# First batch's queries and keys in 1 KB runs, window values for four heads per load, other planner numbers

## The chip, the cores and the metric

The kernel runs on one core of one Trainium2 chip. The metric is device time in microseconds (us), lower is better. In this text PE is the tensor engine, ACT the scalar engine, DVE the vector engine, POOL the GpSimd engine, and SP the engine that issues all DMA transfers here. Each engine works through its own queue of instructions in the order in which the program wrote them, and waits at an instruction whose inputs or buffers are not ready.

## The reference

Attention over 2 batches, 8 heads, 576 tokens, 64 features, then two feed-forward layers on all 1152 tokens:

```python
q_d = q.reshape(B, H, Sd, 4, D).mean(axis=3)      # k_d and v_d in the same way
out_up = np.repeat(sm_attn(q_d, k_d, v_d), 4, axis=2)
mask = np.abs(pos[:, None] - pos[None, :]) < 4
scores = np.where(mask, scale * np.matmul(q, k.transpose(0, 1, 3, 2)), -1e9)
out_local = np.matmul(softmax(scores), v)
x = (out_up + out_local) as (1152, 512)
h = x @ w_in;   x = (h * np.tanh(softplus(h))) @ w_out       # 512 -> 2048 -> 512
g = x @ w_gate; x = (silu(g) * (x @ w_val)) @ w_out2         # 512 -> 1536 -> 512
```

The weights arrive as 64-bit numbers and are turned into 32-bit ones on the core.

## The kernel before

**Attention.** Heads are taken in pairs, so there are 8 pairs (b, p) of a batch and two heads. `prep` loads queries and keys of a pair (`qk`, line 419; the last 64 tokens of all heads come in `qr`, line 394), transposes them on PE (L453 and L459) into PSUM, and ACT copies the PSUM bank to `qkT` (L464, recorded under the helper's line L222). DVE sums groups of four tokens into `qkd` (L474). `duo` then takes two units of 192 tokens of a pair: on PE the mask and the local scores (L552, L557) and the scores of the sums (L566); on DVE the maxima (L572, L578, L583); on ACT the exponentials (L590); normalising on DVE and ACT (L597 to L614); transposes back on PE (L622, L632) and their copies on ACT (`pt`, `ptd`); then the products with the values (L652 for the sums, L660 for the windows). Every window of 70 tokens that a unit needs has its values in `vw`, loaded for the two heads of the pair (L528, L536). There are 12 duos: for each of three pieces of 384 tokens the four pairs. The result of a duo is 128 rows of `xt`.

**Feed-forward.** The first product (`l1`, L733 to L735: three products of 32-bit halves) can start on a piece of 384 tokens when the four duos of that piece are done and a weight chunk has been converted on DVE and ACT (L295 to L331). The second product reads `G`, which comes from the first by a chain on ACT and DVE (L786 to L802). The products with 512 columns (L927 to L929) belong to the last layer.

**Order of the work.** `Plan` is a list scheduler that runs when the program is built. Every operation has an engine, a duration in us that only steers the order, and a `want` time; each engine takes, of what its inputs and buffers allow, what is wanted first, and the instructions are written in that order. Where the planner finds PE idle before 95 us it writes a product that nobody reads (`warm`, L1043). So the number and the place of these products are fixed in the program and don't depend on what happens on the chip.

Of the kernel before, what the change touches and what calls it, by code (L numbers as in the profile page):

```python
# [20 lines left out]
WIN = 70  # L21
# [3 lines left out]
RING = 6  # L25
# [3 lines left out]
FLIGHT = 5  # L29
COLD = 4.0  # L30
# [6 lines left out]
# High words of a float64: the smallest and the largest whose value float32 can hold.  # L37
# [4 lines left out]
class Ring:  # L42
    """n places for buffers of one kind; each goes to the next that asks when it is free."""
# [35 lines left out]
class Plan:  # L79
    """Orders the work of the engines: each takes, of what its inputs and buffers allow, what is  # L80
    wanted first. The durations (us) only steer that order; Tile sets every wait. spare: work for
    an idle tensor engine, with its first and last time and its duration."""
# [6 lines left out]
    def add(self, eng, fn, deps=(), want=0.0, new=(), use=(), table=None):  # L89
        """eng: {engine: duration}; fn(engine) emits. new: buffers it takes first; use: others it touches."""  # L90
# [75 lines left out]
def attention_moe_kernel(  # L166
# [21 lines left out]
    # ------------------------------------------------------------ pools  # L188
# [28 lines left out]
    def us_mm(n):  # L217
        return n / 2400 + 0.003
# [14 lines left out]
    def buf(pool, shape, dt, tag, n):  # L233
        """A buffer; make() gives its tile, in the operation that takes it."""
# [23 lines left out]
    # ------------------------------------------------------------ weights  # L258
# [82 lines left out]
    # ------------------------------------------------------------ attention  # L341
# [55 lines left out]
    def prep(b, p, w):  # L397
        """Queries and keys of two heads with features on partitions, sums of 4 tokens of all."""
        qk = buf(ld, [128, 2, 4, 2, 64], F32, "qk", 3)
# [29 lines left out]
        for i in range(2):  # L429
            l_q.append(plan.add({E_SP: us_dma(1024, 256)}, ld_main(i), l_q, w - 12, [] if l_q else [qk], [qk] if l_q else []))  # L430
# [649 lines left out]
```

## Time and profile before

| | |
|---|---|
| runs before | 513.38, 513.72, 514.73 us; median 513.72 |
| span of the profiled execution | 513.0 us, from its first instruction to its last |
| time of the profiled execution | not shown apart from its span; the median run lies 0.7 us above the span |
| PE busy | 506.3 us (99%) |
| DVE, ACT, POOL busy | 378.4 (74%), 289.6 (56%), 22.9 us (4%) |
| granted TensorE clock | 0.999 |

PE shows 99% busy because the products of an engine overlap in the record (each lasts longer than the distance to the next one) and because the products that nobody reads count as busy. What PE does with its time is read from the distance between the starts of products in the timeline.

### The profile page before, as it was taken

How to read it: one execution, taken by the hardware profiler on the slowest of the kernel's cores; microseconds unless marked ns; L12 is line 12 of the kernel's file. 1: busy time of each engine (PE TensorE's matmuls, PEld its weight loads, DVE VectorE, ACT ScalarE, POOL GpSimd, SP SyncE). 2: the span in 40 equal slices, each digit the busy share in tenths (PEclk: the TensorE clock that was granted, in tenths of full speed). 3: DMA queues.
4: the chain of work that ended last, by engine and by line, in shares of the span. 5: the costliest groups of instructions: out<-in, count | busy, mean ns of one | idle time of the engine just before them, and what ended most of it. 6: DMA issues, size and time to landing. Idle time of an engine off the chain costs nothing.

```text
span 513.0 us, 9052 instructions
## 1 busy us (share of the span) xinstructions
PE 506.3 (99%) x3518; PEld 473.5 (92%) x3518; DVE 378.4 (74%) x760; ACT 289.6 (56%) x591; POOL 22.9 (4%) x47
## 2 busy tenths in 40 slices
PE   8999999999999999999999999999999999999997
PEld 6786688999999999999999999999998899998885
DVE  2776899999998999999889896767764198732322
ACT  3898989698899897469542544334433344310000
POOL 4420320000000000000000000000000000000000
PEclk9999999999999999999999999999999999999999
DMA  9975444452132332451303154222222023000022
GB/s 172 196 147 114 109 133 138 129 165 82 45 121 54 118 87 76 161 165 41 99 27 123 60 173 136 82 84 84 82 83 82 1 82 124 1 1 0 1 87 97
DMA packets 58618, 48.24 MB, mean 94 GB/s; under 512 B 31056, under 2 KB 53840, under 8 KB 58576
## 3 DMA queue, kind: packets, MB, share of 16 engines
q1 hardware_dynamic: 58576, 47.68, 33.6%
q8 instruction: 27, 0.44, 0.4%
q14 instruction: 15, 0.12, 0.1%
HBM read 45.31 MB, written 2.36 MB: 93 GB/s over the span
## 4 chain that ended last, share of the span: by engine, by line
PE 97%; ACT 1%; DVE 1%; issue 0%
PE b L733 23%; PE b L734 23%; PE b L735 23%; PE b L929 5%; PE b L927 5%; PE b L928 5%; PE warm L1043 2%; PE b L557 2%; PE b L660 2%; PE b L622 2%; PE b L453 2%; PE b L566 1%; PE b L652 1%; PE b L632 1%; PE b L552 1%; ACT qkT L222 1%
## 5 line engine op out<-in xcount | busy, mean ns | idle before, releaser
L733 PE MATMUL b<-xy,wt 128*128 128x384 f32 x480 | 161.0, 336 | 0.0
L735 PE MATMUL b<-xy,wt 128*128 128x384 f32 x480 | 160.4, 334 | 0.0
L734 PE MATMUL b<-xy,wt 128*128 128x384 f32 x480 | 160.3, 334 | 0.0
L733 PEld LDWEIGHTS b<-xy,wt 128*128 128x128 f32 x480 | 90.1, 188 | 0.6 <-issue 0.2
L734 PEld LDWEIGHTS b<-xy,wt 128*128 128x128 f32 x480 | 90.1, 188 | 0.0
L735 PEld LDWEIGHTS b<-xy,wt 128*128 128x128 f32 x480 | 90.1, 188 | 0.0
L733 PE MATMUL b<-G,wt 128*128 128x384 f32 x192 | 64.1, 334 | 0.0
L734 PE MATMUL b<-G,wt 128*128 128x384 f32 x192 | 64.1, 334 | 0.0
L735 PE MATMUL b<-G,wt 128*128 128x384 f32 x192 | 64.1, 334 | 0.0
L222 ACT ACTIVATE G<-H 128x384 fp32r<-128x384 f32 (+1 forms) x41 | 25.2, 619 | 63.1 <-DVE H L899 40.2
L295 ACT ACTIVATE cw<-raw 128x512 f32<-128x512 f32 x60 | 39.8, 669 | 21.5 <-DVE wt L331 12.1
L331 DVE TENSOR_TENSOR wt<-cw,wt 128x512 fp32r<-128x512 f32 x68 | 46.1, 684 | 1.2
L310 DVE SCALAR_TENSOR_TENSOR cw<-raw,cw 128x512 uint32<-128x512 uint32 x68 | 46.6, 688 | 0.4
L315 DVE SCALAR_TENSOR_TENSOR cw<-raw,cw 128x512 uint32<-128x512 uint32 x68 | 46.3, 684 | 0.4
L899 DVE TENSOR_TENSOR H<-b,H 128x384 f32<-128x384 f32 x36 | 20.0, 557 | 32.8 <-PE b L735 32.2
L929 PE MATMUL b<-wt,G 128*128 128x512 f32 x108 | 42.1, 389 | 0.0
L928 PE MATMUL b<-wt,G 128*128 128x512 f32 x108 | 42.0, 389 | 0.0
L927 PE MATMUL b<-wt,G 128*128 128x512 f32 x108 | 42.0, 389 | 0.0
L942 DVE TENSOR_TENSOR acc<-b,acc 128x512 f32<-128x512 f32 x18 | 12.4, 692 | 34.6 <-PE b L929 34.6
L896 ACT ACTIVATE H<-b 128x384 f32<-128x384 f32 x36 | 17.6, 489 | 34.5 <-PE b L735 34.5
L735 PEld LDWEIGHTS b<-G,wt 128*128 128x128 f32 x192 | 36.0, 188 | 0.0
L734 PEld LDWEIGHTS b<-G,wt 128*128 128x128 f32 x192 | 36.0, 188 | 0.0
(85 smaller groups left out, 783.7 us busy)
## 6 DMA issues: line engine op xcount, KB each, us to landing
raw<-in_moe_w_out_dram SPq DMA_DIRECT2D x28, 512.0 KB
raw<-in_moe_w_in_dram SPq DMA_DIRECT2D x16, 512.0 KB
raw<-in_moe_w_gate_dram SPq DMA_DIRECT2D x12, 512.0 KB
raw<-in_moe_w_val_dram SPq DMA_DIRECT2D x12, 512.0 KB
vq<-in_v_dram SPq DMA_DIRECT2D x8, 288.0 KB
out_dram<-acc SPq DMA_DIRECT2D x9, 256.0 KB
qk<-in_q_dram SPq DMA_DIRECT2D x8, 256.0 KB
qk<-in_k_dram SPq DMA_DIRECT2D x8, 256.0 KB
```

What stands on the lines that cost most here:

```text
L222: ACT.activation(out, in_, AF.Copy)
L295: ACT.activation(cw.tile, h.bitcast(F32), AF.Abs)
L310: DVE.scalar_tensor_tensor(out=c, in0=words()[:, :, 0], scalar=29, in1=c, op0=ALU.logical_shift_right, op1=ALU.bitwise_or)
L315: DVE.scalar_tensor_tensor(out=c, in0=words()[:, :, 1], scalar=0xC0000000, in1=c, op0=ALU.bitwise_and, op1=ALU.bitwise_or)
L331: DVE.tensor_tensor(out=wt.tile[:, 1], in0=cw.tile, in1=wt.tile[:, 0].bitcast(F32), op=ALU.subtract)
L733: PE.matmul(out=ps, lhsT=wt_hi, rhs=m_hi, start=first, stop=False)
L734: PE.matmul(out=ps, lhsT=wt_hi, rhs=m_lo, start=False, stop=False)
L735: PE.matmul(out=ps, lhsT=wt_lo, rhs=m_hi, start=False, stop=last)
L899: DVE.tensor_tensor(out=h.tile[:, cs], in0=pv.tile[:, 0:n], in1=h.tile[:, cs], op=ALU.mult)
L927: PE.matmul(out=ps.tile, lhsT=g[:, 0, tok], rhs=wt[:, 0], start=(f == fs[0]), stop=False)
L928: PE.matmul(out=ps.tile, lhsT=g[:, 0, tok], rhs=wt[:, 1], start=False, stop=False)
L929: PE.matmul(out=ps.tile, lhsT=g[:, 1, tok], rhs=wt[:, 0], start=False, stop=(f == fs[-1]))
```

## The change

- `prep`, loads: for batch 0 (`KB`) a partition holds four tokens of a head side by side, so a run in memory is 1 KB instead of 256 bytes.
- `prep`, PE: with that layout the two heads no longer stand side by side, so a transpose of 128 columns becomes two products with the identity, one for each head, each writing 64 partitions. Batch 1 keeps its transposes.
- `prep`, ACT: the copy from PSUM to `qkT` runs over the destination in order and reads PSUM with a step of 128 elements; before, it read in order and wrote with a step of four elements.
- `load_windows`: the values of a window are loaded once for four heads (two pairs), in a ring of 12 buffers, instead of per unit and pair.
- Numbers of the planner: a product is priced 0.0103 us higher, the attention's PE work is priced higher, the first products of pieces 0 and 1 are wanted 10 us after the piece's start instead of 20.
- `sub`, `exp_all` and `sums` are added but not called (`whole` is False everywhere).

```diff
     def us_mm(n):
-        return n / 2400 + 0.003
+        return n / 2400 + 0.0133
...
-                nc.sync.dma_start(out=qk.tile[:, i],
-                                  in_=(q, k)[i][b, hs, 0:512].rearrange("h (p r) d -> p r h d", r=4))
+                t, src = qk.tile[:, i], (q, k)[i][b, hs, 0:512]
+                if b in KB:
+                    nc.sync.dma_start(out=t.rearrange("p (h f) -> p h f", h=2), in_=src.rearrange("h (p r) d -> p h (r d)", r=4))
+                else:
+                    nc.sync.dma_start(out=t.rearrange("p (r h d) -> p r h d", r=4, h=2), in_=src.rearrange("h (p r) d -> p r h d", r=4))
...
-                    PE.transpose(out=t[:, 128 * r:128 * r + 128], in_=qk.tile[:, i, r].rearrange("p h d -> p (h d)"), identity=ident)
+                    if b not in KB:
+                        PE.transpose(out=t[:, 128 * r:128 * r + 128], in_=qk.tile[:, i, 128 * r:128 * r + 128], identity=ident)
+                        continue
+                    for h in range(2):
+                        a = 256 * h + 64 * r
+                        PE.matmul(out=t[64 * h:64 * h + 64, 128 * r:128 * r + 128], lhsT=qk.tile[:, i, a:a + 64], rhs=ident,
+                                  start=True, stop=True)
...
-                    copy(e, qkT.tile[:, i, 0:512].rearrange("p (j r) -> p r j", r=4),
-                         ps[i].tile.rearrange("p (r j) -> p r j", r=4))
+                    copy(e, qkT.tile[:, i, 0:512].rearrange("p (j r) -> p j r", r=4),
+                         ps[i].tile.rearrange("p (r j) -> p j r", r=4))
...
+    def load_windows(b, y, ts, w):
+
+        for t in ts:
+            vw = buf(ld, [WIN, 4, 64], F32, "vw", 12)
+
+            def f(e, t=t, vw=vw):
+                nc.sync.dma_start(out=vw.make(), in_=v[b, 4 * y:4 * y + 4, ks_of(t):ks_of(t) + WIN].rearrange("h p d -> p h d"))
+
+            wins[b, y, t] = (vw, plan.add({E_SP: us_dma(4 * WIN, 256)}, f, [], w, [vw]))
...
-            l1(f, i, t + (20 if i < 2 else 0.0) + f * ((t_p1 - t_p0) / RING if i == 0 else (t_p2 - t_p1) / RING if i == 1 else GROUP_US))
+            l1(f, i, t + (10, 10, 0)[i] + f * ((t_p1 - t_p0) / RING if i == 0 else (t_p2 - t_p1) / RING if i == 1 else GROUP_US))
```

How the order moves. On PE, before, from the first pair's scores on (`masks` and `qkT` are the first pair's, `qr` the remainders, `wsrc` the operand of the products that nobody reads):

```order
L552 LDWEIGHTS identb
L552 MATMUL b_200<-masks,identb 128x210
L557 MATMUL b_200<-qkT_160 64x70 x6
L459 MATMUL b_212<-ident,qr_153 128x64 x2
L552 LDWEIGHTS identb
L552 MATMUL b_215<-masks,identb 128x210
L557 MATMUL b_215<-qkT_160 64x70 x6
L1043 LDWEIGHTS wsrc
L1043 MATMUL warm<-wsrc 128x256
```

On PE, now, the rows from the second pair's queries to the first pair's scores (L462 are the new half transposes, `qk_156` the second and `qk_186` the third pair, L548, L553 and L562 what was L552, L557 and L566):

```order
L462 MATMUL b_202<-ident,qk_156 64x128 x8
L462 MATMUL b_216<-ident,qk_156 64x128 x8
L469 MATMUL b_230<-ident,qr_146 128x64 x2
L462 MATMUL b_236<-ident,qk_186 64x128 x8
L462 MATMUL b_160<-ident,qk_186 64x128 x8
L469 MATMUL b_170<-ident,qr_146 128x64 x2
L548 LDWEIGHTS identb
L548 MATMUL b_190<-masks,identb 128x210
L553 MATMUL b_190<-qkT_159 64x70 x6
L562 MATMUL b_190<-qkd_211 64x144 x2
L548 LDWEIGHTS identb
L548 MATMUL b_202<-masks,identb 128x210
```

Three pairs are now transposed ahead of the first scores, and no product that nobody reads stands between them; over the whole program these fall from 90 to 28, 17 of them ahead of the second pair and the other 11 behind the first L636 (what was L622).

On SP, before, from the first values of windows (`vw`) on (`vq` are the values that POOL sums, `qk_167` is batch 1's first pair):

```order
L536 DMA vw_345<-in_v_dram 70x2x64
L528 DMA vw_345<-in_v_dram 70x2x64 x2
L419 DMA qk_167<-in_q_dram 128x8x64
L419 DMA qk_167<-in_k_dram 128x8x64
L528 DMA vw_441<-in_v_dram 70x3x64 x2
L425 DMA vq_272<-in_v_dram 72x4x256
```

On SP, now, the same stretch (`qk_156` is batch 1's first pair):

```order
L424 DMA qk_156<-in_q_dram 128x8x64
L429 DMA vq_179<-in_v_dram 72x4x256
L424 DMA qk_156<-in_k_dram 128x8x64
L429 DMA vq_213<-in_v_dram 72x4x256
L515 DMA vw_305<-in_v_dram 70x4x64
L515 DMA vw_320<-in_v_dram 70x4x64
L515 DMA vw_328<-in_v_dram 70x4x64
L515 DMA vw_330<-in_v_dram 70x4x64
L395 DMA qr_146<-in_q_dram 64x8x64
L395 DMA qr_146<-in_k_dram 64x8x64
L515 DMA vw_367<-in_v_dram 70x4x64
L515 DMA vw_379<-in_v_dram 70x4x64
```

The windows' values now stand behind batch 1's first pair, and two of the six that the first duo of a pair reads stand behind the second load of `qr`.

## Rows read from the trace of the kernel before

**Rows 1.** The page: its first line and the line of PE (busy us, share of the span, instructions).

```profile
span 513.0 us, 9052 instructions
PE 506.3 (99%) x3518; PEld 473.5 (92%) x3518; DVE 378.4 (74%) x760; ACT 289.6 (56%) x591; POOL 22.9 (4%) x47
```

**Rows 2.** The page's costliest groups: one line of each kind of product. Lines 734 and 735 have the same counts as 733, and 927 and 928 as 929.

```profile
L733 PE MATMUL b<-xy,wt 128*128 128x384 f32 x480 | 161.0, 336 | 0.0
...
L733 PE MATMUL b<-G,wt 128*128 128x384 f32 x192 | 64.1, 334 | 0.0
...
L929 PE MATMUL b<-wt,G 128*128 128x512 f32 x108 | 42.1, 389 | 0.0
```

**Rows 3.** PE in order of time (start, duration, engine, line), two stretches: the first three rows lie around the first products with `G`, and from the first to the second there are 21 products; the last two rows lie at the end of the program, with 18 products from one to the other.

```profile
136.06 0.33 PE L733 MATMUL b<-xy,wt 128*128 128x384 f32 x1
...
139.71 0.33 PE L733 MATMUL b<-xy,wt 128*128 128x384 f32 x1
...
140.75 0.33 PE L733 MATMUL b<-G,wt 128*128 128x384 f32 x1
...
504.82 0.39 PE L929 MATMUL b<-wt,G 128*128 128x512 f32 x1
...
508.90 0.39 PE L929 MATMUL b<-wt,G 128*128 128x512 f32 x1
```

**Rows 4.** PE in order of time in the first 28 us (start, duration with the overlap into the next row, line, count).

```profile
1.18 3.38 PE L1043 MATMUL warm<-wsrc 128*128 128x256 bf16 x15 [1.18 <-DVE wsrc L376]
4.54 1.08 PE L453 MATMUL b<-ident,qk 128*128 128x128 f32 x4
5.42 2.00 PE L1043 MATMUL warm<-wsrc 128*128 128x256 bf16 x9
7.25 0.60 PE L453 MATMUL b<-ident,qk 128*128 128x128 f32 x4
...
9.55 0.33 PE L459 MATMUL b<-ident,qr 64*128 64x64 f32 x2
9.82 0.26 PE L552 MATMUL b<-masks,identb 128*128 128x210 bf16 x1
...
10.53 0.39 PE L1043 MATMUL warm<-wsrc 128*128 128x256 bf16 x2
...
13.08 0.71 PE L566 MATMUL b<-qkd 64*64 64x144 f32 x8
13.72 0.61 PE L1043 MATMUL warm<-wsrc 128*128 128x256 bf16 x4
...
22.98 0.49 PE L622 MATMUL b<-ident,ex 128*70 128x128 f32 x3
...
23.63 0.49 PE L622 MATMUL b<-ident,ex 128*70 128x128 f32 x3
...
24.18 0.38 PE L1043 MATMUL warm<-wsrc 128*128 128x256 bf16 x2
...
25.81 0.73 PE L652 MATMUL b<-ptd,vd 72*64 72x64 f32 x16
26.32 0.57 PE L660 MATMUL b<-pt,vw 70*64 70x64 f32 x12
26.82 1.09 PE L453 MATMUL b<-ident,qk 128*128 128x128 f32 x8
27.84 0.46 PE L566 MATMUL b<-qkd 64*64 64x144 f32 x4
```

**Rows 5.** All instructions of the products that nobody reads (count, min/median/max duration in ns, first and last start).

```profile
L1043 PE MATMUL warm<-wsrc x90: 272/273/421, 1.2 to 52.3; 128*128 128x256 bf16 x90
```

**Rows 6.** Busy time of each engine in stretches of the span (stretch, its length; busy us and instructions of PE, PE's weight loads, DVE, ACT, POOL; granted clock, busy share of the DMA engines, GB/s).

```profile
0.00:20.00 20.00, 18.71 (x168) 14.24 (x168) 7.63 (x21) 10.65 (x26) 9.84 (x30) 1.00 1.05 185
20.00:60.00 40.00, 39.37 (x581) 29.80 (x580) 30.91 (x91) 37.59 (x152) 9.79 (x14) 1.00 0.67 136
60.00:140.00 80.00, 78.97 (x746) 73.26 (x743) 75.20 (x169) 67.29 (x166) 3.29 (x4) 1.00 0.40 115
140.00:240.00 100.00, 100.00 (x579) 100.00 (x578) 93.82 (x161) 82.82 (x96) 0.00 (x0) 1.00 0.34 106
```

**Rows 7.** Groups of ACT in the first 105 us by shape (out<-in, count | busy us, mean ns of one | idle before it, and what ended it): copies from PSUM.

```profile
L222 ACT ACTIVATE qkT<-b 128x512 f32<-128x512 f32 x16 | 17.7, 1121 | 6.7 <-PE b L453 6.7
L222 ACT ACTIVATE pt<-b 70x384 f32<-70x384 f32 x24 | 11.8, 502 | 3.2 <-PE b L622 3.0
...
L222 ACT ACTIVATE ptd<-b 72x512 f32<-72x512 f32 x12 | 7.3, 605 | 0.4 <-PE b L632 0.4
```

**Rows 8.** The longest wait of ACT in the first 30 us (us in total, times, longest).

```profile
ACT qkT L222 <- PE b L453: 6.7, 5, 3.7
```

**Rows 9.** SP in order of time: issues of DMA transfers (start, duration of the issue).

```profile
0.73 0.73 SPq L419 DMA_DIRECT2D qk<-in_q_dram  x1
...
2.25 0.87 SPq L394 DMA_DIRECT2D qr<-in_q_dram  x1
...
14.85 0.42 SPq L536 DMA_DIRECT2D vw<-in_v_dram  x1
...
55.76 0.41 SPq L278 DMA_DIRECT2D raw<-in_moe_w_in_dram  x1
```

**Rows 10.** DVE in order of time: the last of the four `G` that the first block of the second product reads.

```profile
137.05 1.36 DVE L802 TENSOR_TENSOR G<-H,G 128x1152 fp32r<-128x1152 f32 x1 [0.39 <-ACT G L222]
```

More of the change, by code (lines that the diff above doesn't have):

```diff
@@ L29 @@
 FLIGHT = 5
+KB = (0,)
 COLD = 4.0
@@ L492, in attention_moe_kernel, with windows, duo @@
     x_ops, in_turn = {}, []
-    def duo(units, i, p, ws):
+    wins = {}
+    def windows(b, y, t):
+        return wins[b, y, t]
+    def load_windows(b, y, ts, w):
[4 more added lines that the diff above has]
+            wins[b, y, t] = (vw, plan.add({E_SP: us_dma(4 * WIN, 256)}, f, [], w, [vw]))
+    def duo(units, i, p, ws, whole):
         LW = 3 * WIN
@@ L503, in duo @@
         mks = [masks[:, (0, 1, 3)[u]:(0, 1, 3)[u] + 3, :] for _, u in units]
-        vw = [buf(ld, [WIN, 2, 3, 64], F32, "vw", 4) for _ in two]
+        vw = [[windows(b, p // 2, t) for t in tiles[k]] for k, (b, u) in enumerate(units)]
         flight = Buf(ring(None, "flight", 5))
@@ L514, in duo @@
         hs = slice(2 * p, 2 * p + 2)
-        def loads(k, w):
-            b, u = units[k]
-            ks = [ks_of(t) for t in tiles[k]]
-            runs = [(0, 3)] if u == 1 else [(0, 1), (1, 2)] if u == 0 else [(0, 2), (2, 1)]
-            t = vw[k]
-            def ld_w(j, n, h):
-                def f(e):
-                    if j == h == 0:
-                        t.make()
-                    s_ = v[b, 2 * p + h, ks[j]:ks[j] + WIN]
-                    nc.sync.dma_start(out=t.tile[:, h, j:j + n],
-                                      in_=bass.AP(tensor=s_.tensor, offset=s_.offset, ap=[[D, WIN], [64 * D, n], [1, D]]))
-                return f
-            def ld_w2(j):
-                def f(e):
-                    if j == 0:
-                        t.make()
-                    nc.sync.dma_start(out=t.tile[:, :, j], in_=v[b, hs, ks[j]:ks[j] + WIN].rearrange("h p d -> p h d"))
-                return f
-            l_w = []
-            for j, n in runs:
-                for fn, m_ in ([(ld_w2(j), 2)] if n == 1 else [(ld_w(j, n, h), n) for h in range(2)]):
-                    l_w.append(plan.add({E_SP: us_dma(m_ * WIN, 256)}, fn, l_w[-1:], w - 5, [] if l_w else [t], [t] if l_w else []))
-            return l_w
         def s_local(k):
@@ L592, in exps, with sub, f, exp_all @@
             return f
+        def sub(k):
+            def f(e):
+                t = m.tile
+                DVE.tensor_tensor(out=ex.tile[:, k, 0:LW].rearrange("p (t j) -> p t j", j=WIN),
+                                  in0=b_s[k].tile[:, 0:LW].rearrange("p (t j) -> p t j", j=WIN),
+                                  in1=t[:, k, 0:3].unsqueeze(2).to_broadcast([128, 3, WIN]), op=ALU.subtract)
+                DVE.tensor_scalar(out=ex.tile[:, k, LW:EW], in0=b_s[k].tile[:, LW:EW], scalar1=t[:, k, 3:4],
+                                  scalar2=0.0625, op0=ALU.subtract, op1=ALU.mult)
+            return f
+        def exp_all(e):
+            ACT.activation(ex.tile, ex.tile, AF.Exp, scale=0.125)
+        def sums(e):
+            DVE.tensor_reduce(out=m.tile[:, :, 4:7], in_=ex.tile[:, :, 0:LW].rearrange("p k (t j) -> p k t j", j=WIN),
+                              axis=AX.X, op=ALU.add)
+            DVE.tensor_reduce(out=m.tile[:, :, 7:8], in_=ex.tile[:, :, LW:EW], axis=AX.X, op=ALU.add)
         def norm(k0, k1):
@@ L685, in duo @@
         add = plan.add
-        l_w = [loads(k, ws[k]) for k in two]
+        l_w = [[y[1] for y in vw[k]] for k in two]
+        vb = [[y[0] for y in vw[k]] for k in two]
         o6 = []
@@ L698, in duo @@
         w = ws[1]
+        if whole:
+            o6 = [add({"ACT": us_act(2 * EW)}, exp_all, o6, w, use=[m, ex], table="exp")]
+            o6 = [add({"DVE": us_tt(2 * LW) + us_tt(2 * SD)}, sums, o6, w, use=[m, ex])]
         if 1 & 1:
@@ L719, in duo @@
         for k in two:
[L720 removed]
+            o15.append(add({E_PE: 0.48}, o_local(k), [o12[k], o14[0]] + l_w[k], w, use=[b_o, pt[k]] + vb[k]))
         o16 = add({"ACT": 0.15}, up_, o14, w, use=[b_o, up])
@@ L960, in attention_moe_kernel @@
         prep(0, p, w)
-        duo([(0, 0), (0, 1)], 0, p, (w, w + 2))
+        if p % 2 == 0:
+            load_windows(0, p // 2, range(6), w)
+        duo([(0, 0), (0, 1)], 0, p, (w, w + 2), False)
         w += 2 * 2
```

35 lines of the change are left out of this document (21 added, 14 removed).

## The prediction

> **What bounds the kernel now.** I read the page first, then PE in order of time at the end of the program, in its middle and at its start, then the engines by stretches, and at last ACT's groups. The page says that PE is busy for 99% of a span of 513.0 us [rows 1]. Is that work or overlap? The end of the program shows it: 18 products of 512 columns start within 4.08 us, one each 0.2267 us, and the last starts at 508.90; in the middle 21 products of 384 columns start within 3.65 us, one each 0.1738 us [rows 3]. There are 1440 and 576 products of 384 columns (three lines of 480 and of 192) and 324 of 512 [rows 2], so the feed-forward layers take 2016 x 0.1738 + 324 x 0.2267 = 423.8 us of PE. PE works from 1.18 [rows 4] to 508.90 + 0.23 = 509.1 us, which is 507.9 us; 84.1 us are left for attention and for waiting.
>
> Attention's own work comes from the starts in [rows 4]. A pair costs 1.02 us for its eight transposes (26.82 to 27.84) and 0.27 for the remainders (9.55 to 9.82): 1.29, and 10.3 for eight pairs. A unit's mask and local scores take 0.71 (9.82 to 10.53), the sums' scores of two units 0.64 (13.08 to 13.72), a unit's transposes back 0.55 (23.63 to 24.18), a duo's products with the sums 0.51 (25.81 to 26.32), a unit's with the windows 0.50 (26.32 to 26.82). A duo is 1.42 + 0.64 + 1.10 + 0.51 + 1.00 = 4.67, and twelve are 56.0. Together 66.3, so PE waits for 17.8 us of the 84.1, and most of these are hidden under 90 products that nobody reads [rows 5].
>
> Where does it wait? Ahead of the first transposes back at 22.98 stand four pairs (5.2 us), six units (4.3) and three times the sums' scores (1.9): 11.4 us of work in the 21.8 us from 1.18 on. So 10.4 us are lost before 22.98, and 7.4 after it. The last unread product stands at 52.3 [rows 5]; from 140 to 240 us PE is busy without a gap [rows 6]. From the middle on the end is set by PE's work alone: what the change saves of waiting before about 100 us comes off the end, and what it adds to PE's work is paid, if it isn't done where PE waits now. That is so as long as DVE keeps up, which is busy for 75.2 of the 80 us from 60 to 140 and 93.8 of the next 100 [rows 6].
>
> **The change part by part.**
>
> *Half transposes.* Batch 0's 32 transposes become 64 products, each in two passes (as L660's six products of a unit are recorded as twelve [rows 4]). 16 passes stand for one tile of queries or keys instead of four. A pass of 128 columns takes 0.109 us (from 7.25 to 7.69 there are four [rows 4]). If the halves of two heads don't overlap, a tile costs 16 x 0.11 = 1.76 us; if they overlap as pairs without any loss, 0.88. The nearest row is L660, which also writes the two halves by turns: 12 passes of 64 columns take 0.50; alone they would be 0.055 each, so six pairs are 0.33 and 0.17 goes into the change of the array's layout. I take 0.88 + 0.17 = 1.05 against 0.51 now: 8 x 0.54 = 4.3 us more PE work (3.0 to 10).
>
> *Loads in 1 KB runs, and the products taken out between them.* The first queries are there at 4.54 at the latest (issued at 0.73 [rows 4, 9]); I take 4.2, with 4.54 as the other end. Until 7.25 PE runs at half rate: the first four transposes take 0.88 us, those at 7.25 take 0.44 [rows 4], so at the 1.2 GHz level against 2.4, though the granted clock is shown as 1.00 [rows 6]. Then I walk through the new order. First pair: at 2.1 us a tile 1.45 tiles are done by 7.25, the other 0.55 by 7.8; remainders 0.27, five unread products 0.55: 8.65. Second and third pair 2.1 + 0.27 each: 13.4. First pair's two units, 1.42 + 0.64: 15.45. Fourth pair: 17.8. Second duo's units: 19.8. One unit more, 1.03: 20.9. Batch 1's first pair, 1.02: 21.9. There the transposes back begin, at 22.98 now. What stands ahead is one unit less (1.03) and one pair's transposes more (1.02): equal. So 1.1 us are won, with the 4.3 us of half transposes already paid. This holds if neither loads nor ACT are late. ACT waited 6.7 us for transposes in this stretch [rows 8], and its copies of a pair are asked for 2.4 us apart. The fewer runs leave room on the DMA engines, which are full in the first 20 us (1.05 of them busy [rows 6]).
>
> *Evictions in order.* A copy to `qkT` takes 1.121 us for 512 elements; the copy `ptd` reads as many elements from PSUM, reads and writes in order, and takes 0.605 [rows 7]. No row shows a read with a step. Its bounds: 0.605 if a read with a step costs nothing, and 1.121 + 0.516 = 1.64 if it costs twice what the stepped write cost. I take 0.61: `pt` at 0.502 for 384 elements shows that reading PSUM runs per element, so nothing but the step in the write tells the two copies apart. Eight copies fall into 20 to 60 us, where ACT is busy for 37.6 of 40 [rows 6]: 4.1 us less ACT work where ACT is nearly full. With that, and with first products that fill PE's gaps earlier, I let the 7.4 us of later waiting fall by half, 3.7; the ends are 0 and 6.2 (all but eleven unread products at 0.109).
>
> The rule that speaks against this part is in the Trainium skill, Advanced Engine Details and Errata, Memory Cachelines: SBUF works in lines of 16 bytes and PSUM in lines of 8, and an access that goes to another line each time pays. A write with a step of four 32-bit numbers is that case, and 1.121 against 0.605 agrees; by the same rule the stepped read of PSUM pays too, and the sum loses most of the 3.7. No run here shows that read yet.
>
> *Window values for four heads.* 64 loads become 36, with as many bytes. An issue takes about 0.4 us of SP [rows 9], so SP has room. The first six windows now stand behind batch 1's first pair, two of them behind the `qr` loads, which wait for the fourth pair's remainders at 17.8; with 0.87 us for each `qr` issue [rows 9] they are issued by 20.5. The first product that reads them comes at about 25 (21.9, two times transposes back 1.10, eleven unread products 1.2, 0.27, 0.51). Before, the values were issued at 14.85 and read at 26.32. I take nothing; if they are late it is a few us once. The first weights stood in SP's queue until 55.76 [rows 9]; now three of their loads stand right behind the second set of windows, so conversion can start earlier.
>
> *Sum.* 513.0 - 1.1 - 3.7 = 508.2 us of span. The median of the runs is 0.7 above the span; the profiled execution's own time isn't shown, so I add 0.7: 508.9, and forecast **508.9**.
>
> **The rivals.**
>
> *PE's later gaps close almost fully.* The new order puts products of the first layer between the duos and no unread ones after the first duo. For it: ACT fills 37.6 of 40 us and is relieved. Against: DVE is at 75 of 80. Then 6.2 instead of 3.7, and tiles at 0.88, 1.4 less: 505.0.
>
> *The eviction keeps its price.* The rule of the Trainium skill named above would give this case. ACT stays nearly full from 20 to 60; for it: the stepped write cost 0.516 by itself, against: no row shows a stepped read. The start is not touched, since PE's walk is full, and of the 3.7 some 0.5 stay: 512.1.
>
> *DVE takes it back.* The fourth `G` that the first block of the second product needs is ready at 138.41, and PE reads the block from 140.75 on [rows 3, 10]: 2.3 us of slack, with DVE at 94%. If DVE gains only 1 us in its idle time before 60 us, and the conversion of one more weight chunk, which the new order puts ahead, costs 2, the block can start at 139.4 and PE keeps 140.75 - 139.4 = 1.35 us: 513.7 - 1.35 = 512.4. Against: DVE is idle 9 us from 20 to 60 [rows 6], and the weights come earlier.
>
> *Slower: the stepped read costs more than the stepped write.* At 1.64 us, ACT's copies of four pairs take 8 x 1.64 = 13.1 us from about 6 us on, with the remainders' copies and two units' exponentials between them; the last ends behind 22, and the start loses its 1.1. From 20 to 60 ACT gets 8 x 0.52 = 4.2 us more where it is full: 513.7 + 4.2 = 517.9. It decides from about 1.26 us a copy, where 8 x 0.14 eats the 1.1.
>
> *Not what it says.* If loads or the queue of SP set the pace at the start, fewer runs help nothing, and PE waits where the unread products stood; it is within the second and third case.
>
> **How the numbers follow.** Forecast as it stands 0.42 (its own range 507 to 511.3), gaps closed 0.18, eviction unchanged 0.16, DVE 0.12, slower 0.12. A measurement of this kernel can tell about 0.3%, 1.5 us, from no change. Faster by more (below 512.2): 0.42 + 0.18 + half of 0.16 + 0.02 = 0.70. Slower by more (above 515.2): 0.12 and 0.01 of the rest, 0.13. Within: 0.17. For 8 in 10 the range leaves out most of the slower case and the lower half of the best one: 504.5 to 514.5.
>
> **What would show it.** The group of `qkT` at about 0.6 us shows the eviction right, at 1.1 or more the rivals. The distance from the second pair's first half transpose to its remainders should be 2.1 us; near 3.5, the halves don't overlap. The first transposes back should start near 22 us. If DVE took it back, PE shows a gap ahead of the first products with `G`. If the forecast is wrong by more than its range, the likeliest place is the stretch from 20 to 100 us, where I halved the waiting by judgement.

## The result, and the profile after

The changed kernel takes 519.18 us (median of four runs, 518.05 to 521.44), against 514.09 for the kernel before beside it: a ratio of 1.0106, interval 1.0093 to 1.0119. It is 5.1 us slower; 508.9 was forecast, with 514.5 as the upper end of the range. The profiled execution of the changed kernel took 519.62 us, 517.8 of them span, so 4.8 us more span than [rows 1].

The page of the changed kernel, its first line, the busy time of PE and DVE, and the shares of the chain that ended last:

```profile
span 517.8 us, 9058 instructions
...
PE 502.9 (97%) x3552; PEld 470.9 (91%) x3552; DVE 380.2 (73%) x762; ACT 281.2 (54%) x589; POOL 23.2 (4%) x47
...
PE 84%; DVE 7%; DMA 4%; ACT 4%; SPq 1%; issue 0%; ACTq 0%
```

PE is busy for less time than in [rows 1], in a longer span, and the chain that ended last, which lies on PE for 84% now and for 97% before, has DVE, DMA and ACT in it. So PE stands still more. What it waits for, by line and releaser (us in total, times, longest):

```profile
PE b L636 <- DVE ex L619: 2.3, 2, 1.7
PE b L674 <- ACT up L680: 2.0, 6, 0.3
PE b L469 <- DMA qr<-in_k_dram: 1.4, 1, 1.4
PE b L755 <- DVE G L823: 1.3, 1, 1.3
...
PE b L462 <- DMA qk<-in_q_dram: 1.0, 1, 1.0
PE b L756 <- DVE wt L332: 0.5, 1, 0.5
PE b L636 <- ACT ex L626: 0.5, 1, 0.5
PE b L666 <- ACT ptd L223: 0.3, 1, 0.3
PE b L458 <- DVE xs L684: 0.3, 1, 0.3
PE b L562 <- DVE m L568: 0.2, 1, 0.2
```

Beside a wait of 1.2 us for the first unread product, which both kernels have ("unread" is short for the products that nobody reads), the same view of the kernel before has two lines: 1.0 us for `up` and 0.7 for `ex`. The start on PE (start, duration, line, count; in brackets the wait and its releaser), which answers [rows 4]:

```profile
3.85 2.94 PE L462 MATMUL b<-ident,qk 128*64 128x128 f32 x32
...
8.36 0.27 PE L469 MATMUL b<-ident,qr 64*128 64x64 f32 x1 [1.37 <-DMA qr<-in_k_dram]
...
9.22 1.97 PE L462 MATMUL b<-ident,qk 128*64 128x128 f32 x32
11.12 0.33 PE L469 MATMUL b<-ident,qr 64*128 64x64 f32 x2
12.41 1.97 PE L462 MATMUL b<-ident,qk 128*64 128x128 f32 x32 [0.96 <-DMA qk<-in_q_dram]
...
23.14 0.49 PE L636 MATMUL b<-ident,ex 128*70 128x128 f32 x3 [0.52 <-ACT ex L626]
```

A pair's half transposes take 1.90 us (9.22 to 11.12), 0.95 a tile. The first transposes back start at 23.14; they stood at 22.98 in [rows 4]. So the start neither won nor lost (0.16 us), and the rest comes behind it. ACT's groups by shape (count | busy us, mean ns | idle before) answer [rows 7]:

```profile
L223 ACT ACTIVATE qkT<-b 128x512 f32<-128x512 f32 x16 | 9.3, 609 | 7.7 <-PE b L462 7.7
L223 ACT ACTIVATE ptd<-b 72x512 f32<-72x512 f32 x12 | 7.2, 596 | 0.3 <-PE b L646 0.3
```

The eviction takes 0.609 us, as taken. Two stretches around a wait on PE near 54 us, in order of time, and then the engines in them and from 110 to 150 us (stretch, length, busy us of PE, weight loads, DVE, ACT, POOL; granted clock, DMA share, GB/s):

```profile
51.44 0.58 PE L553 MATMUL b<-qkT 64*64 64x70 f32 x12
53.69 0.82 PE L636 MATMUL b<-ident,ex 128*70 128x128 f32 x3 [1.67 <-DVE ex L619]
```
```profile
50.00:53.60 3.60, 2.02 (x34) 1.47 (x30) 3.57 (x8) 3.08 (x13) 2.41 (x3) 1.00 0.11 17
53.70:57.00 3.30, 3.30 (x17) 1.96 (x19) 2.29 (x7) 2.47 (x12) 0.00 (x0) 0.50 0.73 225
110.00:150.00 40.00, 38.71 (x224) 38.32 (x223) 35.80 (x57) 39.74 (x43) 0.00 (x0) 1.00 0.21 70
```

PE stood 1.67 us for DVE, and behind that its granted clock is 0.5, the lower of its two levels (1.2 GHz instead of 2.4), for 3.4 us: work for 1.7 us at full rate was lost. From 110 to 150 us ACT is full (35.7 of the 40 us in the kernel before).

After the first transposes back, PE works until 513.65 + 0.23, which is 490.7 us, against 486.15 before (22.98 to 509.13). With the same work behind that point, the 7.4 us of later waiting have become 12.0: 6.9 in the waits listed behind that point (1.7 before), 1.7 from the clock (none), 1.2 under 11 unread products (2.6 under 24), and about 2.2 that are left over, in gaps too short to be listed (3.1). Of the 6.9 us, 5.1 are waits of attention's own steps for DVE and ACT, 1.3 are for a `G` and 0.5 for a weight; the 1.7 before are all attention's.

Last, the order of three events towards the second layer: the end of attention's last block (DVE), ACT's first function on a finished chunk of the first layer, and the fourth `G`. Of the kernel before (the fourth `G` is in [rows 10]):

```profile
98.51 0.55 DVE L680 TENSOR_TENSOR xy<-xs,xy 128x384 fp32r<-128x384 f32 x1
```
```profile
102.53 1.17 ACT L786 ACTIVATE T<-H 128x1152 f32<-128x1152 f32 x1
```

and of the changed one:

```profile
105.89 0.55 DVE L694 TENSOR_TENSOR xy<-xs,xy 128x384 fp32r<-128x384 f32 x1
140.47 1.35 DVE L823 TENSOR_TENSOR G<-H,G 128x1152 fp32r<-128x1152 f32 x1
```
```profile
109.76 1.17 ACT L807 ACTIVATE T<-H 128x1152 f32<-128x1152 f32 x1
```

Attention's fourth block ended 8 us sooner (49.6 against 57.5), its last one 7.4 us later, ACT's functions start 7.2 later, and the fourth `G` is ready at 141.8 instead of 138.4. PE's one wait for a `G` is for the third of them, which is ready at 137.68:

```profile
136.33 1.35 DVE L823 TENSOR_TENSOR G<-H,G 128x1152 fp32r<-128x1152 f32 x1
```
```profile
137.73 0.44 PE L755 MATMUL b<-G,wt 128*128 128x384 f32 x1 [1.29 <-DVE G L823]
```

### The profile page after: what moved, and what is told of

Same layout as the page of the kernel before. It is cut to its first block, busy times and chain, and to the rows that moved or that the text cites. A ratio compares the mean times of both kernels' runs of the same rounds, so it can differ in the third digit from the quotient of the medians.

```text
span 517.8 us, 9058 instructions
## 1 busy us (share of the span) xinstructions
PE 502.9 (97%) x3552; PEld 470.9 (91%) x3552; DVE 380.2 (73%) x762; ACT 281.2 (54%) x589; POOL 23.2 (4%) x47
## 4 chain that ended last, share of the span: by engine, by line
PE 84%; DVE 7%; DMA 4%; ACT 4%; SPq 1%; issue 0%; ACTq 0%
PE b L754 21%; PE b L756 21%; PE b L755 21%; PE b L949 5%; PE b L950 5%; PE b L948 5%; DMA qk<-in_q_dram 1%; PE b L553 1%; DMA raw<-in_moe_w_in_dram 1%; PE b L636 1%; DMA vq<-in_v_dram 1%; PE b L674 1%; PE b L562 1%; PE b L462 1%; PE b L666 1%; ACT T L813 1%
## 5 line engine op out<-in xcount | busy, mean ns | idle before, releaser
L223 ACT ACTIVATE G<-H 128x384 fp32r<-128x384 f32 (+1 forms) x40 | 23.9, 604 | 64.7 <-DVE H L920 43.9
L296 ACT ACTIVATE cw<-raw 128x512 f32<-128x512 f32 x57 | 38.2, 673 | 22.8 <-DVE wt L332 16.3
L223 ACT ACTIVATE wt<-cw 128x512 fp32r<-128x512 f32 x40 | 24.3, 626 | 27.5 <-PE b L755 25.1
```

The lines of the kernel that those rows point to most:

```text
L223: ACT.activation(out, in_, AF.Copy)
L296: ACT.activation(cw.tile, h.bitcast(F32), AF.Abs)
```

## The experiments

The first theory was that the loss is DVE's order: first-layer products that are wanted sooner pull weight conversions ahead of attention's steps on DVE, and PE waits. The rivals: the half transposes' work is simply paid; the unread products that are gone (28 instead of 90) let the clock fall. A conversion turns a chunk of 64-bit weights into 32-bit ones. With each time below stands its ratio to the kernel before, run beside it, and that ratio's interval.

### The changed kernel with one thing undone

First products wanted late again:

```diff
-  t + (10, 10, 0)[i] + ...
+  t + (20, 20, 0)[i] + ...
```

> The changed kernel, with the first layer's products wanted 20 us after the start of their stretch again, instead of 10. Theory (DVE's order): the sooner products pull the first weights' conversions ahead of attention's steps on DVE, so PE waits for DVE from 50 us on; with the old wants some of the conversions stand later, and the time falls from 519.2 to between 514.5 and 517. Rival A (the half transposes' work is simply paid, 3.5 us): 518.5 to 520, since they are all still there. Rival B (the unread products that are gone let TensorE's clock fall): 28 of them stand in this kernel as in the changed one, so 518.5 to 520, with a stretch of granted clock 0.5 near 54 us.

526.72 us, 1.0236 (1.0205 to 1.0267): 7.5 us slower still. The theory's first half falls. The fourth `G` is at 152.8, and PE stands 4.8 us for `G` from 130 us on. The granted clock is 0.5 in three stretches, 17 us in all (from 13, 54 and 133 us on), which is up to 8.5 us of work at full rate; the changed kernel lost 1.7 that way.

The planner's old prices:

```diff
-  return n / 2400 + 0.0133
+  return n / 2400 + 0.003
...
-  E_PE: (1.06 if b in KB else 0.5) if i < 2 else 0.24
+  E_PE: 0.44 if i < 2 else 0.11
...
-  E_PE: 0.66 ... 0.34 ... 0.37 ... 0.25
+  E_PE: 0.58 ... 0.27 ... 0.33 ... 0.22
```

> The changed kernel, with the planner's old prices for PE's work (0.003 instead of 0.0133 in each product, 0.44, 0.11, 0.58, 0.27, 0.33 and 0.22 for attention's). 78 unread products stand in it instead of 28. Theory (DVE's order): the first conversion ends after the sixth attention block's last step on DVE instead of ahead of it, so the wait of 1.7 us near 54 us and a part of what follows goes: 516 to 518.5. Rival A (half transposes' work): they are priced too low, but done as before: 518.5 to 520. Rival B (unread products): no stretch of granted clock 0.5, 517 to 518.

516.59 us, 1.0054 (1.0039 to 1.0069): 2.6 us gained, no clock drop. Prices that only steer the order are worth as much as any operation so far, but without the new ones the changed kernel still stands 2.7 us above the kernel before.

Batch 0 loaded in short runs and transposed whole:

```diff
-KB = (0,)
+KB = ()
```

> The changed kernel without the 1 KB runs: batch 0's queries and keys come in runs of 256 bytes and are transposed whole. Rival A (their work is paid in full): 3.5 us less PE work, 515.2 to 516.2. Theory (DVE's order): the conversions still stand early, and PE waits for DVE where it no longer transposes: 517.5 to 520. Rival B (59 unread products instead of 28): 517 to 518.5.

516.32 us, 1.0046 (1.0029 to 1.0063): 2.9 gained, somewhat under the 3.5 of work. It fits the rival that the work is paid, but leaves 2.4 us over the kernel before. The planner made a new order here too.

### Each part alone, the planner making its order

The eviction, put into the kernel before:

```diff
-  copy(e, qkT...rearrange("p (j r) -> p r j", r=4), ps...rearrange("p (r j) -> p r j", r=4))
+  copy(e, qkT...rearrange("p (j r) -> p j r", r=4), ps...rearrange("p (r j) -> p j r", r=4))
```

> The kernel before with nothing changed but the eviction: the copies to qkT read PSUM with a step and write in order. The order of all instructions is the one of before. If ACT is what the waiting from 20 to 60 us hangs on, 8 copies at 0.51 us less there give 2 to 4 us: 510 to 512. If DVE's order sets PE's waiting, as the theory says, 513.2 to 514.2. Either way the group of qkT should take 0.61 us a copy instead of 1.12.

512.85 us, 0.9981 (0.9972 to 0.9991). Prices and order are those of before, and every event from the first block to the fourth `G` (136.4) comes 1 to 2 us sooner. It is the base for what follows. To it are added: 1 KB runs with half transposes, these and their loads at their true price, then the sooner wants alone:

```diff
+KB = (0,)
...
-  E_PE: 0.44 if i < 2 else 0.11
+  E_PE: (1.0 if b in KB else 0.44) if i < 2 else 0.11
```

> The kernel before with the eviction in order and batch 0's 1 KB runs with half transposes, priced as they are; the windows' loads, the first products' wants and the other prices as before. The eviction alone gave 512.85. If the half transposes' 3.5 us are paid in full and nothing else follows, 516 to 517; if PE waits there anyway, 512.5 to 514; if their longer stretch on PE moves the planner's order so that conversions stand ahead of the sixth block, as in the changed kernel, 517 to 523.

521.55 us, 1.0157 (1.0135 to 1.0179): 8.7 us over the eviction alone, far more than 3.5. PE waits 4.4 us for `G` from 124 us on.

```diff
-  t + (20 if i < 2 else 0.0) + ...
+  t + (10 if i < 2 else 0.0) + ...
```

> The kernel before with the eviction in order and the first layer's products wanted 10 us after the start of their stretch instead of 20; loads, transposes and prices as before. The eviction alone gave 512.85. The run with the old wants in the changed kernel was 7.5 us slower, so sooner products do not harm there. If they fill PE's gaps as the prediction had it, 509.5 to 512; if they pull conversions ahead of attention on DVE, 513.5 to 516.

513.87 us, 0.9997 (0.9988 to 1.0007): 1.0 over the eviction alone. Filling PE's gaps with sooner products gained nothing. And the window loads with a new order (the changed kernel with short runs, old prices and old wants):

> The changed kernel without the 1 KB runs, with the old wants and the old prices: of the change, the eviction in order and the window loads for four heads are left. The planner makes a new order of it, with 103 unread products and the first conversion ahead of the sixth attention block. If the loads are worth nothing by themselves and the order doesn't matter: 512 to 513.5, as the eviction alone. If a new order costs what it does in the other kernels, because conversions stand ahead of attention's steps on DVE: 515 to 519.

519.96 us, 1.0116 (1.0101 to 1.0131): 7.1 over, with waits of 3.4 us for `G`. Parts that cost 8.7, 1.0 and 7.1 alone cost 6.3 together, with the new prices beside them. They don't add up, so it is hardly the operations alone that cost.

### The same operations in the old order

The planner can be left with the old prices and the old list of work while other instructions are emitted; then every engine but SP keeps the order of before. Half transposes first:

```diff
+KB = (0,)
...
   E_PE: 0.44 if i < 2 else 0.11
```

> The kernel before with the eviction in order and batch 0's 1 KB runs with half transposes, but with the planner's old prices for both, so that every engine keeps the order of the kernel before (all 90 unread products too). It tells the half transposes' own cost from the order that the planner makes of them: the same change with true prices took 521.55, and the eviction alone 512.85. If their 3.5 us of PE work are paid: 515.5 to 517. If they fit where PE waited in the first 23 us: 512 to 513.5. If the cost lies in the work and not in the order: above 519.

517.65 us, 1.0077 (1.006 to 1.0093): 4.8 over the eviction alone. PE at the start:

```profile
10.04 0.39 PE L1053 MATMUL warm<-wsrc 128*128 128x256 bf16 x2
10.36 1.09 PE L462 MATMUL b<-ident,qk 128*64 128x128 f32 x16
11.38 0.33 PE L469 MATMUL b<-ident,qr 64*128 64x64 f32 x2
11.65 1.16 PE L1053 MATMUL warm<-wsrc 128*128 128x256 bf16 x9
```

PE has no gap here: the unread products run at their place though real work stands behind them, so the longer transposes come on top. The next run leaves 36 of them out:

```diff
   def warm(e):
+      said.append(1)
+      if 15 < len(said) <= 51:
+          return
       PE.matmul(...)
```

> The half transposes in the old order (517.65 with all 90 unread products) without 36 of the first 51 unread products, 3.9 us of PE. They run in their place in PE's order whether PE is late or not, so in the old order the half transposes came on top of them. If half transposes can stand in the time of the unread products, as the prediction's walk through the start had it: 512.5 to 514. If loads or ACT set the pace of the start: 515.5 to 518, with PE waiting where the unread products stood, and the granted clock perhaps at half.

513.5 us, 0.9994 (0.9985 to 1.0003): 4.15 us come back for 3.9 us of unread products. In the old order the half transposes fit into the time of these unread products, and then cost 0.65 over the eviction alone. Now the window loads, emitted where the first load of two pairs stood:

```diff
-  nc.sync.dma_start(out=t.tile[:, :, j], in_=v[b, hs, ...])
+  if j == h == 0 and p % 2 == 0:
+      for a in range(3):
+          nc.sync.dma_start(out=wtile4(w4 + k, a), in_=v[b, 2 * p:2 * p + 4, ...])
```

> The kernel before with the eviction in order and the window values loaded for four heads (36 loads instead of 64), put where the first load of the two pairs stood, while the planner still reckons with the old loads: every engine but SP keeps the order of the kernel before. The same loads with a new order took 519.96, the eviction alone 512.85. If the loads themselves are worth nothing: 512.3 to 513.5. If they are late or crowd the DMA queue: above 515, with waits of PE for vw.

513.32 us, 0.9989 (0.9979 to 0.9998): 0.5 over the eviction alone, which is within the intervals, where the new order took 7.1. And all three together, with the same 36 unread products left out:

> All three changed operations (eviction in order, 1 KB runs with half transposes, window loads for four heads) in the order of the kernel before, without 36 of the first 51 unread products. Only the prices, the wants and the order that comes of them differ from the changed kernel's 519.18. If the loss beyond the half transposes' work is the order's: 512.5 to 515. If the operations cost by themselves what the changed kernel lost: 517 to 520.

513.91 us, 0.9996 (0.9987 to 1.0005). The three add up (512.85 + 0.5 + 0.65 = 514.0), and this is 5.3 us less than the changed kernel with the same operations. What PE waits for in it, the first row being the wait for the first unread product:

```profile
PE warm L1060 <- DVE wsrc L377: 1.2, 1, 1.2
PE b L634 <- DVE ex L617: 0.7, 1, 0.7
PE b L569 <- ACT qkT L223: 0.5, 1, 0.5
PE b L672 <- ACT up L678: 0.3, 1, 0.3
```

Behind it stand three short waits instead of ten lines. The counterpart changes no operation at all, only the changed kernel's prices on the eviction alone:

```diff
-  return n / 2400 + 0.003
+  return n / 2400 + 0.0133
...
-  E_PE: 0.44 if i < 2 else 0.11
+  E_PE: 0.5 if i < 2 else 0.24
...
-  E_PE: 0.58 ... 0.27 ... 0.33 ... 0.22
+  E_PE: 0.66 ... 0.34 ... 0.37 ... 0.25
```

> The kernel before with the eviction in order and the changed kernel's prices for PE's work, and nothing else: no operation is changed, but the planner makes a new order, with 52 unread products instead of 90 and other places for the conversions. If the order matters as much as the operations: 515 to 519. If prices nearer to the real durations make a better order: 510 to 512.5. If it makes no difference: 512.5 to 513.5.

518.62 us, 1.0099 (1.0084 to 1.0114): 5.8 us lost by prices alone. PE, then DVE's fourth `G`, then the engines behind PE's wait:

```profile
125.10 0.44 PE L733 MATMUL b<-G,wt 128*128 128x384 f32 x1 [2.71 <-ACT G L222]
126.55 0.69 PE L734 MATMUL b<-G,wt 128*128 128x384 f32 x1 [1.01 <-DVE G L802]
```
```profile
143.57 1.35 DVE L802 TENSOR_TENSOR G<-H,G 128x1152 fp32r<-128x1152 f32 x1
```
```profile
125.50:132.20 6.70, 5.69 (x19) 5.66 (x19) 6.70 (x10) 6.64 (x8) 0.00 (x0) 0.50 0.18 59
```

In this order attention ends sooner than before (91.5), but ACT's first function comes at 112.7: counted on PE, 173 first-layer products start ahead of it, instead of 95. The fourth `G` is at 144.9, and the granted clock is 0.5 for the 6.7 us shown.

### DVE's work, conversions, and the clock

No conversion ahead of the sixth attention block:

```diff
-  mag, [o_load, prev.get("mag")], w0, ...
+  mag, [o_load, prev.get("mag") or x_ops[1, 1]], w0, ...
```

> The changed kernel, with one more dependency for the planner: the first weight's conversion starts only when the sixth of the twelve attention blocks is written. No conversion stands ahead of the seventh block on DVE then, as in the kernel before; 28 unread products as in the changed one. Theory (conversions ahead of attention's steps on DVE make PE wait from 50 to 70 us): the 1.67 us wait, the clock drop and the waits to 70 us go, some 3 to 5 us: 514 to 516.5. Rival (DVE's work has to be done anyway, and what isn't converted by then is missed near 135 us, where PE waits for G): 518 to 520, with a longer wait ahead of the second layer's first products.

517.51 us, 1.007 (1.0047 to 1.0093): 1.7 gained by the medians of 3 to 5 expected, with single runs from 515.3 to 520.7. The waits near 54 and 62 us are gone, the one for `G` stays (1.4 us). In its trace the clock drop has moved: it comes at 28 us, behind 1.7 us of waiting for `qr`. Then DVE's work itself, without the clamp of the weights to the range of 32-bit numbers, which is left out of the kernel in the changed order and in the old one:

```diff
   def range_(e):
-      c = cw.tile
-      DVE.tensor_scalar(out=c, in0=c, scalar1=LOW64, scalar2=TOP64, ...)
+      pass
```

> The changed kernel, in the same order, without the clamp of the weights to float32's range (L302, one DVE instruction of 0.42 us a chunk, 68 of them; that part of the computation is left out). DVE has 0.42 us less to do in each conversion, some 6 us by the 14th chunk, and nothing else moves. Theory (PE's waiting from 50 to 140 us hangs on DVE, which does conversions between attention's steps): the waits near 53, 62, 68 and 136 us shrink or go, with the clock drop: 513 to 516. Rivals (DMA at the start, ACT's copy ahead of the window products, the half transposes' work): 518 to 520.

> The control for the run before: the kernel before with the eviction in order, in its old order, and the same clamp left out. The eviction alone took 512.85 and shows one wait for DVE (0.7 us near 59 us) and no drop of the clock. Theory (in the old order DVE is nearly as full, but hardly ahead of PE): 511.5 to 513. If DVE bounds this order as much as the changed one, it gains as much as that: 508 to 511.

519.41 us, 1.0108 (1.0082 to 1.0133), and 513.25, 0.999 (0.9981 to 0.9999). Neither gains. By the fourth `G` the clamp takes DVE 6.7 us in the changed order (16 chunks) and 5.9 in the old (14). Without it that `G` is ready 1.6 us sooner in the changed order (140.2) and no sooner in the old (136.6). Even the 1.6 are not the clamp's alone: in this trace the first transposes back start 1.7 us sooner (21.48), PE waits 2.1 us for `qr` near 25 us, and the clock drop comes at 28 us. What fits the theory is that the wait at 54 us shrinks from 1.67 to 0.61. ACT is as full as with the clamp:

```profile
110.00:150.00 40.00, 38.71 (x223) 38.35 (x223) 34.45 (x51) 39.73 (x43) 0.00 (x0) 1.00 0.21 66
```

So DVE's load by itself is not the bound. That it is DVE's place in a chain of PE, ACT and DVE fits this, and was not tested. The clock next: 14 unread products ahead of the wait at 53.69 us:

```diff
+  if (p, i, k) == (1, 1, 0):
+      o10.warm = 14
...
+  for _ in range(getattr(o, "warm", 0)):
+      self.spare[0].fn(e)
   o.fn(e)
```

> The changed kernel with 14 more products that nobody reads, put on PE ahead of the transposes back that wait 1.67 us for DVE at 53.69 us. No other instruction moves. If the drop of the granted clock behind that wait (53.7 to 57.1 us, passes at double length) is what the unread products that are gone cost, it does not come, some 3.4 us of work are done in 1.7, and the time falls from 519.2 to 517 to 518. If the clock is no cause, or DVE sets the pace behind it anyway, 518.5 to 519.7.

523.48 us, 1.0168 (1.0126 to 1.021), between 519.1 and 524.1. This run decides nothing: in its trace PE waits 2.4 us for the loads of `qr` at 23 us and 1.9 for `ptd` at 49.4, ahead of the products put in, and the clock falls anyway. The same idea where it can be read, in the kernel with the prices alone:

```diff
+  if not begun:
+      begun.append(1)
+      for _ in range(24):
+          plan.spare[0].fn(e)
   wt, g = wts["2", f].tile, G[f].tile
```

> The kernel with the prices alone (518.62), with 24 unread products (2.6 us) more on PE, right ahead of the first product that reads G, where PE stood 2.71 us. No other instruction moves. If the drop of the granted clock (125.4 to 132.2 us, a product of 384 columns in 0.32 us instead of 0.174) comes of the standing, it doesn't come, and 6.8 us of work at half rate are done in 3.4: 515 to 516. If the clock falls for another reason, or PE waits for G behind it anyway: 518 to 519.

518.83 us, 1.0092 (1.0075 to 1.0109): no gain. PE, then the stretch that had the clock drop:

```profile
122.40 2.80 PE L1049 MATMUL warm<-wsrc 128*128 128x256 bf16 x24
...
126.71 0.44 PE L734 MATMUL b<-G,wt 128*128 128x384 f32 x1 [1.00 <-DVE G L802]
...
138.87 0.45 PE L733 MATMUL b<-G,wt 128*128 128x384 f32 x1 [0.62 <-DVE G L224]
140.60 0.44 PE L734 MATMUL b<-G,wt 128*128 128x384 f32 x1 [1.28 <-DVE G L802]
```
```profile
125.50:132.20 6.70, 5.70 (x33) 5.50 (x33) 6.70 (x10) 6.65 (x7) 0.00 (x0) 1.00 0.20 73
```

The clock stays at 1.00, PE is ahead by what it saved, and gives it back waiting for `G` at 138 and 139 us. In this order the clock drop cost nothing: the `G` come as late without it (the fourth at 145.1, 144.9 with it).

### Unread products in the eviction's kernel

```diff
   def warm(e):
+      said.append(1)
+      if 33 < len(said) <= 999:
+          return
       PE.matmul(...)
```

> The eviction alone (512.85), in the old order, without the unread products from the 34th on (57 of 90, 6.2 us of PE; the first 33 stand ahead of some 8 us). If unread products hold up work that is ready: 508 to 511.5. If PE only waits where they stood: 512.5 to 513.5. If the granted clock falls where PE waits now: 513.5 to 517, with more spread between runs.

510.59 us (509.4 to 511.65), 0.993 (0.991 to 0.9949): 2.3 us better than the eviction alone, and faster than both kernels of this case. PE now waits where it had been filled, for a load:

```profile
17.16 0.63 PE L453 MATMUL b<-ident,qk 128*128 128x128 f32 x4 [2.34 <-DMA qk<-in_q_dram]
```
```profile
18.60:21.90 3.30, 3.30 (x31) 2.38 (x27) 2.63 (x7) 1.84 (x9) 2.07 (x4) 0.50 1.03 205
```

The clock is at half for 3.4 us behind that wait, and the run wins all the same. It also changes how the run with all operations is read: that run was set beside an eviction kernel with all its unread products. Beside this one its operations cost 3.3 us, about the work of the half transposes, though it has 21 unread products more. The eviction alone with the same 36 left out was not run.

### What the runs have in common

The first column is the median of the runs; the others are read from the profiled execution, in us.

| kernel | us | last block | first function on ACT | fourth `G` | last product starts |
|---|---|---|---|---|---|
| before | 514.1 | 99.1 | 102.5 | 138.4 | 508.9 |
| changed | 519.2 | 106.4 | 109.8 | 141.8 | 513.7 |
| wants late | 526.7 | 99.8 | 120.2 | 152.8 | 521.2 |
| half transposes alone | 521.6 | 94.7 | 99.0 | 144.7 | 514.4 |
| window loads alone | 520.0 | 95.8 | 99.7 | 144.3 | 513.6 |
| prices alone | 518.6 | 91.5 | 112.7 | 144.9 | 512.6 |
| eviction alone | 512.9 | 97.1 | 100.6 | 136.4 | 506.9 |
| all operations, old order | 513.9 | 99.0 | 102.2 | 138.1 | 508.6 |
| eviction, fewer unread | 510.6 | 95.9 | 99.4 | 135.3 | 505.8 |

In all 20 traces the last product starts 367.6 to 372.0 us after the fourth `G` is ready, while that point moves from 135.3 to 152.8. The slow orders are late there, each in its own way: the changed kernel by a late end of attention, the prices alone, by the counts on PE, through products put ahead of the ones that ACT needs. Which choice of the planner makes each of them late was not tried.

The fourth `G` is a mark here and not yet a cause. In the old order no trace lists a wait of PE for a `G`, and both the mark and the end come later with what PE lost ahead of them. In the changed kernel the mark moves by 3.4 us and the end by 4.8. The slow orders, except the one with the old prices and the one kept busy, also have stretches of granted clock 0.5, 3.4 to 17 us in a trace. What these are worth was tried in the order of the prices alone.

## Why the prediction was wrong

**The step that failed** is the term of later waiting, "I let the 7.4 us of later waiting fall by half, 3.7", which the prediction itself called judgement. It rose to 12.0, and 8.3 of the 9.6 us between the predicted span (508.2) and the measured one are in it. The reasoning behind it was that each part, if it is faster, shortens the waiting of the old order. But the prices and wants are part of the change too, and they made another order. Prices alone lost 5.8 us on the eviction's kernel; all operations in the old order, with 36 unread products left out, took the time of the kernel before. The prediction priced instructions, and read the order of PE only for the first 22 us. The last 0.7 us between the forecast and the median are the step from span to time: 0.7 was added, and the median lies 1.4 above the span.

**Start.** 21.9 was predicted and 23.14 measured, 1.2 of the 9.6. The walk through PE's work held (half transposes 0.95 a tile against 1.05, with as much work ahead as before); the condition "if neither loads nor ACT are late" did not hold: the waits for `qr` (1.37), queries (0.96) and ACT (0.52) are there in the rows.

**Half transposes.** +4.3 us predicted, 8 x (0.95 - 0.51) = 3.5 measured in the work, and the 4.8 of the old order with all unread products bounds it from above. That they are "already paid" at the start holds where unread products make room: in the old order leaving 36 of them out gave 4.15 us back.

**Eviction.** 0.61 us a copy, right. Its worth was not taken apart in the prediction; alone it gives 1.1 us. The prediction took from the Trainium skill (Advanced Engine Details and Errata, Memory Cachelines) that a stepped read of PSUM should pay as the stepped write to SBUF did; what that page says of PSUM is that access that is not contiguous slows matmuls. For ACT's copy the trace shows no such price: 0.609 us with the step in the read, 0.596 for `ptd` without. So the rivals in which the eviction keeps its price, or gets dearer, fall by their own test; the forecast of the second of them, 517.9, was near the result by luck, with a wrong mechanism.

**Window values.** Taken as nothing: 0.5 us in the old order. The prediction saw that with the weights' loads further forward "conversion can start earlier", as a gain; in the trace conversions stand ahead of attention's steps, and moving them back gained 1.7 us by the medians.

**DVE takes it back.** Of the rivals its mechanism came nearest: PE shows a gap of 1.3 us among the first products with `G`, near the place named. But its 2.3 us of slack are misread. In the kernel before, 140.75 [rows 3] is not where PE begins with `G`; its first such product, and one of twelve more, start here:

```profile
125.67 0.33 PE L733 MATMUL b<-G,wt 128*128 128x384 f32 x1
...
138.84 0.33 PE L734 MATMUL b<-G,wt 128*128 128x384 f32 x1
```

Its price (512.4) was too small and its cause too narrow: taking 6.7 us of the clamp from DVE left the time as it was (519.41), with ACT full from 110 to 150 us.

**Settled and open.** Shown: the same operations take 5.3 us more in the changed order than in the old one, and prices alone cost 5.8 us on a kernel whose operations they leave as they are, so most of the loss is the order's; in the order from prices alone the clock drop is no cause. The operations are not free: the half transposes took the time of unread products, 4.8 us over the eviction alone with all of these and 0.65 with 36 left out. For the changed kernel's own clock drop, its two runs at a mean clock of 1.000 took 518.05 and 518.75 and the two at 0.997 took 519.62 and 521.44, so about four of the five us are lost without it. Open: which planner decision would have to be held to keep the changed kernel's wants and prices. These prices explain only a part there, since taking them back gained 2.6 us.

## What to carry to other kernels

Where a planner writes the order, a change of any price or want is a change of the whole program: time the new operations in the old order first, and the new order with the old operations, before judging either. Products that nobody reads keep their place in PE's queue: they hide nothing once real work is ready, and have to be thinned when work is added. Thin them in the kernel of comparison too, or the new work looks free. Look for a point that the end moves with (here the fourth `G`) and compare orders there, not by engines' busy shares; then ask what PE waits for ahead of it.

## What the runs showed of the hardware

A copy by ACT from PSUM with a step of 512 bytes between elements cost next to nothing (0.609 us, against 0.596 for the copy `ptd` without a step), while the stepped write to SBUF had cost 0.516 us more [rows 7].

Unread products delay ready work: 3.9 us of them, left out in the same order, gave 4.15 us. That agrees with the Trainium skill, PSUM — Partial Sum Buffer, Engine vs sequencer instructions, by which matmuls start and complete in program order.

Half products that write the two halves of a bank by turns take little more than half the time of a whole one each: 32 passes of 128 columns in 1.90 us are 0.059 us each, against 0.109 for a pass of a whole transpose [rows 4]. That is what two overlapping halves would give.

Loads at the start land differently from run to run in the same order: the changed kernel waited 1.37 us for `qr` at 7 us, the same order with 14 more unread products (they stand behind 50 us) waited 1.71 and 0.68 at 23 and 25 us. The changed kernel's runs spread over 3.4 us, those of the kernel before over 1.35; that the loads make this spread is not shown.
